# Gated mix of two attentions: single PSUM banks in the query stage, 72 instead of 80 maxima units in the front, and projections between two visits

## The chip, the cores and the metric

The kernel runs on one core of one Trainium2 chip. The metric is the device time of one execution in microseconds; the median of three runs is compared.

## The reference

Both halves get the same `x` of 2048 tokens by 448 columns, with 16 heads of 28.

```python
g = sigmoid((x * gate_w).sum(-1, keepdims=True))
# A: linear attention with a learned feature map
q, k, v = heads(x @ A_wqkv)
pq, pk = q @ w_phi, k @ w_phi                      # per head, 28 x 28
phi = concat([softmax(p), softmax(-p)])            # of pq and of pk: 56 features
kv, z = phi_k^T @ v, phi_k.sum(tokens)
a = ((phi_q @ kv) / (phi_q @ z + 1e-6)) @ A_wo
# B: full softmax attention
q, k, v = heads(x @ B_wqkv)
b = (softmax(q @ k^T * 28**-0.5) @ v) @ B_wo
out = g * a + (1 - g) * b
```

## The kernel before

The program is written for one core. The order of instructions on TensorE (PE), VectorE (DVE), ScalarE (ACT) and GpSimd (POOL) is the order of the Python code, written out by hand; DMAs go through the queue of SyncE (SP), which issues in its own order and waits in place. An engine that waits for one instruction holds all that are behind it.

The 16 heads are four groups `g` of four heads; the 2048 queries are four blocks `qb` of 512. A pair `gq = 4 g + qb` is the unit of attention B, so there are 16 of them, and one takes 16 steps `s` of 128 keys.

**Maxima.** The softmax of B subtracts the maximum of each query's scores over all keys, which has to be known before attention reaches that `gq`. So scores are computed twice, and the first time only their maxima are kept, as columns of `part`, 64 columns to a `gq`. This is done in two ways:

- In the front, as *units* (`mx_unit`, 16 to a `gq`, `NF` = 80 in all, the first five `gq`). A unit makes four matmuls of 512 keys: two into `pmb` (scores of the first block of keys) and two into `pmd` (scores of the difference of two blocks of keys, which `pair_load` prepares: DMAs bring `kp` and `kt`, POOL subtracts, line 189). ACT takes the relu of `pmd` into `rl` (line 245), DVE adds `pmb` and takes the maximum (line 248, two instructions). `rl` has one buffer; `pmb` and `pmd` each take two PSUM banks, from a ring of two such pairs (tag `mx`).
- In attention, as *visits* (`mx_visit`). A visit makes three matmuls of 512 keys into the three banks of `pm` (line 276, one buffer) and one DVE reduction over them (line 287).

When a `gq` is complete, `mx_reduce` reduces its columns on DVE, the next unit or visit transposes them on PE (`mx_done`), and ACT multiplies by -1 into `nm` (line 219). A visit with such a transpose has only two matmuls. A DMA puts `nm` into row 0 of the stack of queries `qst` (line 705, in `load_q`), where attention uses it as one more row of the contraction.

**The front** runs, one after the other:

1. Twenty projections `pqk` of B's queries and keys (line 494), written to DRAM as `qkd`.
2. The *key stage*, `t` from 0 to 15: `pk` (A's keys through the feature map, weights folded in line 326), `pva` (A's values), every second `t` a further `pqk`, and in pairs `kv_add`. A unit stands before and one after `pk`; for `t` of 3, 8 and 13 there is a third at the end (line 633).
3. The *query stage*, `q = t - 16` from 0 to 24. For each of 16 tiles of 128 tokens: `pq` (line 615), then features (`features1`: ACT copies to `pc`, DVE takes maximum and minimum, POOL and, for `q` below 7, DVE subtract in lines 382 and 384; ACT's exp in the next tile; `features2`: DVE's sum and reciprocal, POOL's product in line 395). Three tiles on, `turn` transposes the features on PE into `pft` (line 451), and ACT copies them to `fT` (line 453). Every second tile, `numer` computes numerators and denominators `pn` (line 462); `normalize1` has ACT copy them to `oU` (line 336, two buffers) and DMAs fetch the denominators; `normalize2` (DVE, DMAs) and `normalize3` (DVE, line 356) follow in the next tiles; `normalize4` splits the result into `oT` (ACT line 364, POOL line 365). `out_a` projects it (`poa`), and in the next tile `out_a2` has ACT multiply by the gate and stores it to `gad`. Units stand after `pq`, from `q` = 11 also in every second tile at the end, from `q` = 18 in each. From `q` = 18 on `value_b` computes B's values (`pvb`).
4. The rest of `value_b`, with a unit each, while POOL clears the stacks `qst` and `kst` (lines 691 and 693) and SP loads them. Units left over follow (line 722).

PSUM in the front is one pool of eight banks: three single banks `s` (for `pk`, `pva`, `pqk`, `pq`, `poa`, `pvb` and small ones), one `pv` for `pkv`, and two pairs `mx`, which units share with `pft` and `pn`.

**Attention.** A step makes four score matmuls into two pairs of banks `st` (line 754), two exps on ACT into `p` (line 756), a visit, and `values` (line 766) with `p` of the step before. In the last group (`g` = 3, from step 192) two projections by `woB` are worked in: `project_first` (nine matmuls, `pob_False`) at `kt` of 4, 6, 8 and 10, and `project_last` (three, `pob_True`) eleven steps and more after the end of a `gq`. They take one pair of banks from the ring of `st`. ACT multiplies the result by the gate and POOL adds it (lines 790, 791), or DVE does both (line 783). They stand after `values`; the step with a `project_first` then has a second visit:

```python
        mx_visit()
        if 0 < s <= NS:
            values(s - 1)
            ...
        for fn in late.pop(s, []):
            fn()
        if s in pobs and kt in FIRST:
            mx_visit()
```

Of the kernel before, what the change touches and what calls it, by code (L numbers as in the profile page):

```python
# [23 lines left out]
NG = 4  # L24
# [5 lines left out]
NF = 80  # L30
# [9 lines left out]
def gated_mix_kernel(ctx, tc, xT, wqkB, wvB, wvA, wkAT, wqAT, phi, woA, woB,  # L40
# [103 lines left out]
    mxs = {"u": 0, "f": 4 * NF, "fin": [], "pend": None}  # L144
# [57 lines left out]
    def mx_reduce(gq, n):  # L202

        def reduce():
            red = mxp.tile([P, 16], F32, tag="red", name=f"red{gq}", bufs=2)
            nc.vector.tensor_reduce(
                red.rearrange("p (h t) -> p h t", t=4),
                part[:, 64 * gq:64 * gq + 16 * n].rearrange("p (k t h) -> p h t k", t=4, h=4),
                AX.X, ALU.max)
            mxs["red"], mxs["pend"] = red, gq  # L210

        mxs["fin"].append(reduce)

    def mx_done(pt):

        gq, mxs["pend"] = mxs["pend"], None
        nc.tensor.transpose(pt[:16, :P], mxs["red"], ident)
        nm_of[gq] = nm = mxp.tile([16, P], F32R, tag="nm", name=f"nm{gq}", bufs=7)
        acts.append(lambda: nc.scalar.mul(nm, pt[:16, :P], -1.0))

    def mx_unit():

        u = mxs["u"]
        if u == NF:
            return
        if mxs["pend"] is not None:
            mx_done(ps_s(f"pt{mxs['pend']}"))
# [12 lines left out]
        for j in range(4):  # L240
            js = slice(32 * j, 32 * j + DH)
            nc.tensor.matmul((pb if j < 2 else pd)[:, j % 2, :], qc[js, qt * P:(qt + 1) * P],  # L242
                             kc[js, :], start=True, stop=True, tile_position=(32 * j, 0))
        rl = mxp.tile([P, 2, 512], F32, tag="rl", name=f"rl{u}", bufs=1)
        nc.scalar.activation(rl, pd, AF.Relu)  # L245
        col = 64 * gq + 16 * b + 4 * qt + 2 * hp
        for i in range(2):
            nc.vector.tensor_tensor_reduce(rl[:, i, :], pb[:, i, :], rl[:, i, :], 1.0, LOWEST,  # L248
                                           ALU.add, ALU.max, part[:, col + i:col + i + 1])
        if qt == 3 and gq + 1 == NF // 16:  # L250
            mx_load(g + (qb == NQ - 1), c)
        elif qt == 3 and qb == NQ - 1:
            pair_load(g + 1, c)
        if r == 15:
            mx_reduce(gq, 2)

    def mx_visit():
# [5 lines left out]
        n = min(3 if pend is None else 2, 4 * NU - f)  # L263
        if n <= 0 and pend is None:
            return
        mxs["f"] = f + n
        pm = ps2.tile([P, 3, 512], F32, tag="mx", name=f"pm{f}", bufs=1)
        for i in range(n):
            u, j = divmod(f + i, 4)
            gq, r = divmod(u, 16)  # L270
            g, qb = divmod(gq, NQ)
            kb, qt = divmod(r, 4)
            if r == 4 and j == 0 and gq + 1 < NG * NQ:
                mx_query(gq + 1)
# [6 lines left out]
            if r == 15 and j == 3:  # L281
                mx_reduce(gq, 4)
        if pend is not None:
            mx_done(pm[:, 2, :])
            acts.pop()()
        if n:
            nc.vector.tensor_reduce(part[:, f:f + n], pm[:, :n], AX.X, ALU.max)  # L287
# [45 lines left out]
    def normalize1(pool, pn, nm, n):  # L333

        oU = pool.tile([P, n, 512], F32, tag="oU", name=f"oU{nm}", bufs=2)
        (nc.scalar.copy if n == 2 else nc.vector.tensor_copy)(oU, pn)
# [106 lines left out]
    def turn(u):  # L443
# [4 lines left out]
        pt = ps_mx(f"pft{u}")  # L448
        f = fq.pop(u)
        for n in range(8):  # L450
            nc.tensor.transpose(pt[:112, n // 4, n % 4 * P:(n % 4 + 1) * P],
                                f[:, n * 112:(n + 1) * 112], ident)
        nc.scalar.copy(fT_of[tb][:, :, tl * P:(tl + 1) * P],
                       pt[:112].rearrange("p i (n q) -> p (i n) q", q=P))

    def numer(tb):

        pn = ps_mx(f"pn{tb}")
        for g in range(NG):
            for hh in range(2):  # L460
                n = 2 * g + hh
                nc.tensor.matmul(pn[64 * hh:64 * hh + 64, g // 2, g % 2 * 256:g % 2 * 256 + 256],
# [127 lines left out]
    for i in range(2 * NT + 9):  # L590
# [17 lines left out]
        if t < NT:  # L608
# [3 lines left out]
            mx_unit()  # L612
# [15 lines left out]
        if t < NT:  # L628
# [12 lines left out]
        if q == 2:  # L641
# [5 lines left out]
            kvT = kv_copy()  # L647
            woA_s = weights(3, "woA_s")
# [28 lines left out]
    out_a2(NT - 1)  # L677
    mx_fin()
# [23 lines left out]
    def load_q(gq):  # L702
        g, qb = divmod(gq, NQ)
        qst_of[gq] = r = load_stack(qst[gq % 2], q_d[g], qb * 512, (0, 0, 1, 1))
        nc.sync.dma_start(f32(r[0:1].rearrange("p a b -> p (a b)")), f32(nm_of.pop(gq)))
# [8 lines left out]
    load_q(0)  # L714
    for t in range(7, NT):
# [27 lines left out]
    pv_of, pts, late = {}, {}, {}  # L743
    pobs = set()
# [58 lines left out]
    def finish(gq, s):  # L803
# [5 lines left out]
        def f1():  # L809
            st["n"] = normalize1(late_p, pv_of[gq].unsqueeze(1), f"b{gq}", 1)  # L810
# [19 lines left out]
        if g == NG - 1:  # L830
            for tl in range(4):
                pobs.add(s + 11 + tl)
                late.setdefault(s + 11 + tl, []).append(
                    lambda tl=tl: project_last(qb, st["o"], tl, qb == 2))
# [34 lines left out]
    for s in range(NS + 16):  # L869
        take_acts()  # L870
        if s < NS:
# [21 lines left out]
        if s in pobs and kt in FIRST:  # L893
            mx_visit()
# [68 lines left out]
```

## Time and profile before

| | |
|---|---|
| Timed runs | 1160.21, 1160.40, 1161.12 us, median 1160.4 |
| Profiled execution | 1162.2 us, span 1160.4 us |
| Granted TensorE clock, mean | 0.976 |
| Busy in the span | PE 1092.5, ACT 743.6, DVE 689.0, POOL 248.6 us |
| Key stage, first `pk` to first `pq` | 66.5 to 206.9 us |
| Query stage to its last `out_a` | 206.9 to 399.9 us |
| Last values, to the first `st` of attention | 399.9 to 432.9 us |
| Attention | 432.9 us to the end |

Times within the trace are microseconds from the start of the span. An engine's busy time counts its instructions, not its waits; a matmul's duration overlaps the next one's, so the step from one start to the next is what a matmul costs PE. PEld is the loading of weights, which overlaps PE. In a list of instructions the bracket gives the idle time of the engine ahead of that instruction and what ended it. PEclk is the share of the full TensorE clock that was granted.

### The profile page before, as it was taken

The numbers are of one execution on the slowest core, as the hardware profiler recorded it, in microseconds if no ns is written. First come the engines' busy times: TensorE is split into PE (matmuls) and PEld (weight loads), VectorE is DVE, ScalarE is ACT, GpSimd is POOL, SyncE is SP. The second block draws the span as 40 slices with busy tenths as digits, with TensorE's granted clock in tenths as the row PEclk, the third lists the DMA queues.
The fourth block names the chain that finished last, engine by engine and source line by source line (L and its number), as shares of the span: only waits on it lengthen the run. The fifth ranks groups of instructions, "written<-read, shape, count | busy, mean of one in ns | idle before, by whom it ended". The sixth has DMA issues, their size and how long they took to land.

```text
span 1160.4 us, 16421 instructions
## 1 busy us (share of the span) xinstructions
PE 1092.5 (94%) x6360; PEld 591.2 (51%) x6360; DVE 689.0 (59%) x841; ACT 743.6 (64%) x876; POOL 248.6 (21%) x211
## 2 busy tenths in 40 slices
PE   7999999878889999999999999999999999999997
PEld 5877777656656763334333433333333344444443
DVE  4546767785444446767666676766676666654012
ACT  3445555565555556777777777777777766666763
POOL 1144444445562440011000000000000001121200
PEclk9999999999888998999999999999999999999999
DMA  8863101012122282143353221343322422122301
GB/s 259 297 182 97 46 27 45 19 45 70 45 75 83 83 176 55 39 130 111 74 117 84 66 69 37 80 101 83 88 56 58 115 52 76 40 79 82 118 10 64
DMA packets 64717, 99.56 MB, mean 86 GB/s; under 512 B 15456, under 2 KB 24528, under 8 KB 64640
## 3 DMA queue, kind: packets, MB, share of 16 engines
q1 hardware_dynamic: 64640, 98.52, 30.2%
q8 instruction: 50, 0.82, 0.3%
q14 instruction: 27, 0.22, 0.1%
HBM read 69.54 MB, written 28.57 MB: 85 GB/s over the span
## 4 chain that ended last, share of the span: by engine, by line
PE 81%; DVE 6%; ACT 5%; POOL 3%; issue 3%; DMA 1%; SPq 1%; ACTq 0%; POOLq 0%; DVEq 0%
PE st L754 22%; PE pv L766 21%; PE pm L276 9%; PE pqk L104 6%; PE pva L104 3%; PE pk L104 3%; PE pvb L104 3%; PE pob_False L104 3%; DVE part L287 2%; PE pmb L242 2%; PE poa L104 2%; PE pq L104 2%; POOL oTa L365 1%; PE pob_True L104 1%; ACT rl L245 1%
## 5 line engine op out<-in xcount | busy, mean ns | idle before, releaser
L756 ACT ACTIVATE p<-st 128x1024 f32<-128x1024 f32 x512 | 497.6, 1021 | 160.8 <-PE st L754 159.2
L287 DVE TENSOR_REDUCE part<-pm 128x3 f32<-128x1536 f32 (+1 forms) x239 | 413.3, 1729 | 200.9 <-PE pm L276 179.9
L754 PE MATMUL st<-qst,kst 128*128 128x512 f32 x1024 | 312.7, 424 | 6.0 <-DVE acc L783 2.6
L754 PEld LDWEIGHTS st<-qst,kst 128*128 128x128 f32 x1024 | 173.0, 189 | 231.1 <-ACT p L756 183.8
L766 PE MATMUL pv<-p,vb 128*32 128x512 f32 x2048 | 273.8, 606 | 0.0
L248 DVE CUSTOM_DVE_ANT_0 rl<-pmb,rl 128x512 f32<-128x512 f32 x160 | 103.2, 682 | 76.4 <-ACT rl L245 76.1
L276 PE MATMUL pm<-kc,qc 28*128 28x512 f32 x704 | 120.8, 497 | 9.3 <-DVE part L287 8.7
L245 ACT ACTIVATE rl<-pmd 128x1024 f32<-128x1024 f32 x80 | 82.2, 1028 | 36.2 <-PE pmd L242 32.9
L356 POOL TENSOR_TENSOR oUb<-oUb,rsb 128x512 f32<-128x512 f32 x15 | 19.3, 1283 | 388.8 <-DMA rsb<-rdb 274.7
L276 PEld LDWEIGHTS pm<-kc,qc 28*128 28x128 f32 x704 | 45.0, 182 | 97.8 <-DVE part L287 86.9
L104 PE MATMUL pqk<-XH,wB 128*128 128x512 f32 x224 | 70.9, 409 | 6.7 <-ACT XH L303 6.7
L766 PEld LDWEIGHTS pv<-p,vb 128*32 128x32 f32 x2048 | 40.5, 108 | 65.3 <-issue 60.1
L242 PE MATMUL pmd<-kp,qp 28*128 28x512 f32 x160 | 42.2, 517 | 14.1 <-DVE part L248 8.3
L104 PEld LDWEIGHTS pqk<-XH,wB 128*128 128x128 f32 x224 | 43.3, 196 | 16.3 <-ACT XH L303 6.9
L104 PE MATMUL poa<-woA_s,oTa 128*128 128x448 f32 x192 | 49.0, 409 | 0.1
L242 PE MATMUL pmb<-kp,qp 28*128 28x512 f32 x160 | 40.8, 505 | 6.7 <-ACT rl L245 3.5
L496 ACT CAST ev<-pqk 128x512 fp32r<-128x512 f32 x28 | 16.4, 587 | 46.7 <-PE pqk L104 44.4
L104 PEld LDWEIGHTS poa<-woA_s,oTa 128*128 128x128 f32 x192 | 39.2, 211 | 8.0 <-issue 4.3
L497 DVE TENSOR_TENSOR ev<-pqk,ev 128x512 fp32r<-128x512 f32 x28 | 19.4, 692 | 38.1 <-ACT ev L496 38.0
L104 PE MATMUL pk<-wkA_s,XH 128*128 128x448 f32 x128 | 40.1, 396 | 0.0
L791 POOL TENSOR_TENSOR acc<-acc,ob_False 128x448 f32<-128x448 f32 x12 | 13.7, 1142 | 122.5 <-ACT ob_False L790 122.5
L104 PE MATMUL pq<-wqA_s,XH 128*128 128x448 f32 x128 | 39.7, 393 | 0.0
(132 smaller groups left out, 1111.9 us busy)
## 6 DMA issues: line engine op xcount, KB each, us to landing
qkd<-ev SPq DMA_DIRECT2D x28, 512.0 KB
qst<-qkd SPq DMA_DIRECT2D x64, 224.0 KB
kst<-qkd SPq DMA_DIRECT2D x64, 224.0 KB
od<-oTb SPq DMA_DIRECT2D x12, 512.0 KB
oL<-od SPq DMA_DIRECT2D x12, 512.0 KB
xraw<-in_xT_dram SPq DMA_DIRECT2D x8, 512.0 KB
rsa<-rda SPq DMA_DIRECT2D x16, 256.0 KB
rsb<-rdb SPq DMA_DIRECT2D x15, 256.0 KB
```

The costliest lines, as they stand in the source:

```text
L104: nc.tensor.matmul(dst, l, r, start=i == 0, stop=i == len(todo) - 1)
L242: nc.tensor.matmul((pb if j < 2 else pd)[:, j % 2, :], qc[js, qt * P:(qt + 1) * P], kc[js, :], start=True, stop=True, tile_position=(32 * ...
L245: nc.scalar.activation(rl, pd, AF.Relu)
L248: nc.vector.tensor_tensor_reduce(rl[:, i, :], pb[:, i, :], rl[:, i, :], 1.0, LOWEST, ALU.add, ALU.max, part[:, col + i:col + i + 1])
L276: nc.tensor.matmul(pm[:, i, :], mxs[("qc", gq)][js, qt * P:(qt + 1) * P], mxs[("kc", g, kb)][js, :], start=True, stop=True, tile_position= ...
L287: nc.vector.tensor_reduce(part[:, f:f + n], pm[:, :n], AX.X, ALU.max)
L356: (nc.gpsimd if n == 1 else nc.vector).tensor_mul(oU, oU, rs)
L496: nc.scalar.copy(e[:, 0, :], pq)
L497: nc.vector.tensor_sub(e[:, 1, :], pq, f32(e[:, 0, :]))
L754: nc.tensor.matmul(st[:, jl, :], kst_of[(g, kt // 4)][:, j, (kt % 4) * P:(kt % 4 + 1) * P], qst_of[gq][:, j, :], start=True, stop=True)
L756: nc.scalar.activation(p, st, AF.Exp, scale=SCALE)
L766: nc.tensor.matmul(pv[32 * j:32 * j + 32, :], vb[kt // 8][:, kt % 8, 4 * g + j, :], pt[j // 2][:, j % 2, :], start=kt == 0, stop=kt == NT ...
```

## The change

- `NF` is 72. The front covers four `gq` in the old way and half of the fifth: its eight units take the query tiles `qt` 0 and 1 of all keys, and the visits take the rest (list `flats`, 736 matmuls instead of 704).
- The key stage has no unit before `t` = 2 and no third units; `pair_load` of the third and fourth pair comes at `t` = 1 and 3, and POOL's subtractions (`take_subs`) come behind the features of the tile.
- From `q` = 2 a new PSUM pool `psq` has four single banks and the two pairs. `turn` and `numer` take two single banks each, with one ACT copy for each bank; the pairs are left to the units. The pools wait tile by tile (`reuse_waits="tile"`).
- `oU` has three buffers in the query stage. DVE's share of the features' subtraction goes to POOL for all `q`. `out_a2` follows `out_a` in the same tile. The second unit of a tile stands in each tile from `q` = 14.
- In attention `nm` is multiplied by DVE. Its DMA is taken out of `load_q` (`load_nm`), and comes at `kt` = 12, or 14 for the last two `gq`. The second stack `qst1` is cleared last.
- `project_first` stands between the two visits of its step, ahead of `values`; `project_last` stands there too, and a second visit follows where the maxima are behind a schedule that ends in step 237.

```diff
-NF = 80
+NF = 72
...
-    ps = ps_s_.enter_context(tc.tile_pool(name="ps", bufs=1, space=PSUM))
+    ps = ps1 = ps_s_.enter_context(tc.tile_pool(name="ps", bufs=1, space=PSUM, reuse_waits="tile"))
...
-        return ps.tile([P, 512], F32, tag="s", name=nm, bufs=3)
+        return ps.tile([P, 512], F32, tag="s", name=nm, bufs=3 if ps is ps1 else 4)
...
-    def mx_done(pt):
+    def mx_done(pt, eng):
...
-        acts.append(lambda: nc.scalar.mul(nm, pt[:16, :P], -1.0))
+        if eng is nc.vector:
+            eng.tensor_scalar_mul(nm, pt[:16, :P], -1.0)
+        else:
+            acts.append(lambda: eng.mul(nm, pt[:16, :P], -1.0))
...
-        c, qt = divmod(r, 4)
-        hp, b = divmod(c, 2)
-        if r in (4, 9) and u // 16 + 1 < NF // 16:
-            pair_query(gq + 1, r // 9)
-        if r == 4 and gq + 1 == NF // 16:
-            mx_query(gq + 1)
+        if gq < GM:
+            c, qt = divmod(r, 4)
+            hp, b = divmod(c, 2)
+            col = 64 * gq + 16 * b + 4 * qt + 2 * hp
+            if r in (4, 9):
+                pair_query(gq + 1, r // 9)
+        else:
+            qt, c = divmod(r, 4)
+            hp, b = divmod(c, 2)
+            col = 64 * gq + 8 * b + 4 * qt + 2 * hp
+            if r == 0:
+                mx_query(gq)
...
+    flats = [(GM, kb, qt, h, 64 * GM + 16 + 8 * kb + 4 * (qt - 2) + h)
+             for kb in range(4) for qt in (2, 3) for h in range(4)]
+    flats += [(gq, kb, qt, h, 64 * gq + 16 * kb + 4 * qt + h) for gq in range(GM + 1, NG * NQ)
+              for kb in range(4) for qt in range(4) for h in range(4)]
...
-            mx_done(pm[:, 2, :])
-            acts.pop()()
+            mx_done(pm[:, 2, :], nc.vector)
...
-        oU = pool.tile([P, n, 512], F32, tag="oU", name=f"oU{nm}", bufs=2)
-        (nc.scalar.copy if n == 2 else nc.vector.tensor_copy)(oU, pn)
+        oU = pool.tile([P, n, 512], F32, tag="oU", name=f"oU{nm}", bufs=1 + n)
+        for i in range(n):
+            (nc.scalar.copy if n == 2 else nc.vector.tensor_copy)(oU[:, i, :], pn[i])
...
-        pt = ps_mx(f"pft{u}")
+        pt = [ps_s(f"pft{u}_{i}") for i in range(2)]
...
-        pn = ps_mx(f"pn{tb}")
+        pn = [ps_s(f"pn{tb}_{i}") for i in range(2)]
...
-        take_subs()
-        if t in (0, 1):
-            pair_load(0, 2 + t)
-        if 1 <= t < NT:
+        if 3 <= t < NT:
             mx_unit()
...
-            mx_unit()
+            if t >= 2:
+                mx_unit()
...
-            fq[q] = features1(pq, f"q{q}", nc.vector if q < 7 else nc.gpsimd)
+            fq[q] = features1(pq, f"q{q}", nc.gpsimd)
...
+        if i >= 1:
+            take_subs()
+        if t in (1, 3):
+            pair_load(0, 2 + t // 2)
...
-            if t in (3, 8, 13):
-                mx_unit()
         take_lows()
-        if 0 <= y - 9 < NT:
-            out_a2(y - 9)
...
+            ps_s_.close()
+            ps = ps_s_.enter_context(tc.tile_pool(name="psq", bufs=1, space=PSUM, reuse_waits="tile"))
...
             out_a(y - 8)
+            out_a2(y - 8)
...
-        if q >= NT + 2 or q >= 10 and q % 2:
+        if q >= NT - 2:
             mx_unit()
...
-        nc.sync.dma_start(f32(r[0:1].rearrange("p a b -> p (a b)")), f32(nm_of.pop(gq)))
+    def load_nm(gq):
+        nc.sync.dma_start(f32(qst_of[gq][0:1].rearrange("p a b -> p (a b)")), f32(nm_of.pop(gq)))
...
-    qst = [stack(f"qst{i}", False) for i in range(2)]
+    qst = [stack("qst0", False)]
     kst = [stack(f"kst{i}", True) for i in range(5)]
+    qst.append(stack("qst1", False))
...
+            if kt == (12 if gq + 1 < 14 else 14) and gq + 1 < NG * NQ:
+                load_nm(gq + 1)
...
-            if g == NG - 1 and kt in FIRST:
-                pobs.add(s)
-                late.setdefault(s, []).append(
-                    lambda qb=qb, tl=FIRST.index(kt): project_first(qb, tl, qb == 3))
...
         mx_visit()
+        if s < NS and g == NG - 1 and kt in FIRST:
+            project_first(qb, FIRST.index(kt), qb == 3)
+            mx_visit()
+        if s in mids:
+            mids.pop(s)()
+            if mxs["f"] * 237 < len(flats) * s:
+                mx_visit()
...
-        if s in pobs and kt in FIRST:
-            mx_visit()
```

More of the change, by code (lines that the diff above doesn't have):

```diff
@@ L200, in mx_fin, with mx_reduce @@
             mxs["fin"].pop(0)()
-    def mx_reduce(gq, n):
+    GM = NF // 16
+    def mx_reduce(gq):
+        col = 64 * gq
+        if gq < GM:
+            parts = [(0, 4, col, 2)]
+        elif gq == GM:
+            parts = [(0, 2, col, 2), (2, 4, col + 16, 4)]
+        else:
+            parts = [(0, 4, col, 4)]
         def reduce():
             red = mxp.tile([P, 16], F32, tag="red", name=f"red{gq}", bufs=2)
[L206 to L209, printed above, removed]
+            for a, z, c, n in parts:
+                nc.vector.tensor_reduce(
+                    red.rearrange("p (h t) -> p h t", t=4)[:, :, a:z],
+                    part[:, c:c + 4 * (z - a) * n].rearrange("p (k t h) -> p h t k", t=z - a, h=4),
+                    AX.X, ALU.max)
             mxs["red"], mxs["pend"] = red, gq
         mxs["fin"].append(reduce)
-    def mx_done(pt):
+    def mx_done(pt, eng):
         gq, mxs["pend"] = mxs["pend"], None
@@ L262, in mx_visit @@
         f = mxs["f"]
-        n = min(3 if pend is None else 2, 4 * NU - f)
-        if n <= 0 and pend is None:
+        todo = flats[f:f + (3 if pend is None else 2)]
+        todo = [x for i, x in enumerate(todo) if x[4] == todo[0][4] + i]
+        if not todo and pend is None:
             return
-        mxs["f"] = f + n
+        mxs["f"] = f + len(todo)
         pm = ps2.tile([P, 3, 512], F32, tag="mx", name=f"pm{f}", bufs=1)
-        for i in range(n):
-            u, j = divmod(f + i, 4)
-            gq, r = divmod(u, 16)
+        for i, (gq, kb, qt, j, col) in enumerate(todo):
             g, qb = divmod(gq, NQ)
-            kb, qt = divmod(r, 4)
-            if r == 4 and j == 0 and gq + 1 < NG * NQ:
-                mx_query(gq + 1)
+            if kb == 1 and qt in (0, 2) and j == 0 and gq + 1 < NG * NQ:
+                if ("qc", gq + 1) not in mxs:
+                    mx_query(gq + 1)
             js = slice(32 * j, 32 * j + DH)
@@ L280, in mx_visit @@
                 mx_load(g + 1, kb)
-            if r == 15 and j == 3:
-                mx_reduce(gq, 4)
+            if kb == 3 and qt == 3 and j == 3:
+                mx_reduce(gq)
         if pend is not None:
-            mx_done(pm[:, 2, :])
-            acts.pop()()
+            mx_done(pm[:, 2, :], nc.vector)
+        n = len(todo)
         if n:
-            nc.vector.tensor_reduce(part[:, f:f + n], pm[:, :n], AX.X, ALU.max)
+            col = todo[0][4]
+            nc.vector.tensor_reduce(part[:, col:col + n], pm[:, :n], AX.X, ALU.max)
     bd_s = ExitStack()
@@ L714, in gated_mix_kernel @@
     load_q(0)
+    load_nm(0)
     for t in range(7, NT):
@@ L742, in gated_mix_kernel @@
     NS = NG * NQ * NT
-    pv_of, pts, late = {}, {}, {}
-    pobs = set()
+    pv_of, pts, late, mids = {}, {}, {}, {}
     def scores(s, i):
```

34 lines of the change are left out of this document (16 added, 18 removed).

## The prediction

> **What bounds the kernel now.** I read the page's busy shares, then busy time by window, then the waits and the order in time of the stages that the change touches. The profiled execution took 1162.2 us for a span of 1160.4; the three timed runs have a median of 1160.4, so I sum against 1162.2 and take off 1.8 at the end. A change under 0.2% (2.3 us) counts as none.
>
> ```profile
> PE 1092.5 (94%) x6360; PEld 591.2 (51%) x6360; DVE 689.0 (59%) x841; ACT 743.6 (64%) x876; POOL 248.6 (21%) x211
> ```
>
> ```profile
> 160.00:180.00 20.00, 20.00 (x160) 15.27 (x159) 14.18 (x32) 10.98 (x18) 8.95 (x8) 1.00 0.15 54
> ...
> 240.00:260.00 20.00, 14.78 (x97) 11.11 (x99) 18.75 (x37) 14.25 (x19) 9.59 (x8) 1.00 0.24 64
> ...
> 320.00:340.00 20.00, 16.29 (x78) 11.44 (x77) 11.05 (x26) 10.59 (x15) 11.74 (x11) 0.83 0.21 65
> 340.00:360.00 20.00, 17.62 (x80) 12.10 (x80) 6.04 (x17) 8.68 (x11) 9.57 (x10) 0.76 0.28 91
> ...
> 460.00:480.00 20.00, 20.00 (x120) 7.84 (x118) 13.57 (x9) 15.12 (x16) 0.00 (x0) 1.00 0.10 23
> ```
>
> Columns: length, busy PE, PEld, DVE, ACT, POOL, granted clock. The key stage (66.5 to 206.9) and attention (from 432.9) are PE's. The query stage between is nobody's, except DVE's at 240; its clock sinks to 0.76. What holds it:
>
> ```profile
> ACT oUa L336 <- POOL oTa L365: 18.0, 4, 6.5
> ```
>
> ```profile
> PE pft L451 <- ACT rl L245: 9.2, 8, 1.3
> PE pmd L242 <- DVE part L248: 5.7, 6, 1.4
> ```
>
> ACT copies numerators only when POOL has read the oU two blocks back, and behind it stand the copies of pft; both hold pairs of banks that the maxima need.
>
> **Key stage.** Three extra units (t of 3, 8, 13) stand right before the next unit:
>
> ```profile
> 143.88 0.50 PE L242 MATMUL pmb<-kp,qp 28*128 28x512 f32 x2
> 144.01 0.50 PE L242 MATMUL pmd<-kp,qp 28*128 28x512 f32 x2
> 145.68 0.50 PE L242 MATMUL pmb<-kp,qp 28*128 28x512 f32 x2 [1.17 <-ACT rl L245]
> 147.02 0.50 PE L242 MATMUL pmd<-kp,qp 28*128 28x512 f32 x2 [0.84 <-DVE part L248]
> 147.46 0.67 PE L104 MATMUL pk<-wkA_s,XH 128*128 128x448 f32 x2
> ```
>
> Two take 3.58 us. An undisturbed pair of tiles, 158.18 to 173.51, is 15.33 us: two pk (2.43), two pva (2.45), pqk 2.57, kv_add 0.93 and four units, so 0.52 a unit. At these rates the stage holds 38.9 + 39.2 + 20.6 + 6.5 (seven kv_adds) + 4.2 (folds, one pt) + 34 x 0.52 = 127.1 us; it took 140.35. The 13.2 over are these doubles, 3.2 us in which the first unit's pmd waits for POOL's kp (68.84 to 72.52), and half-rate matmuls behind them. The change has 27 units, the first at t = 2, none doubled: 127.1 - 3.6 = 123.5, gain 16.9. Against that, POOL subtracts kp behind the features, SP's kt of the next pair waits for that, and wtq queues behind kt. Estimate: kp_0 done at 81.3, wtq's first slab at 85, its fold due at 84: 1 us. **Gain 15.5**, bounds 12 and 18.
>
> **Query stage, q 0 to 8** (a tile is one q; 206.86 to the turn at 262.36, 55.5 us). PE needs 9 pq (2.43), 9 units, 6 turns (0.84), 3 numer (1.88), kv_add and pkvT: 38.8. DVE needs 9 times ext 1.15, sum and reciprocal 1.42, unit 1.37, and 9.8 once (last key sum 1.4, ev 0.7, KV 0.7, gates 1.2, two splits of woA 3.4, normalizing 2.3): 45.3. Before, seven L384 of 0.94 made it 51.8; the change gives them to POOL, also at 0.94, whose 3.6 us a tile fit. PE's unit waits for DVE's one before. Taking 47: **gain 8.5** (4 to 11).
>
> **q 9 to 15** (262.36 to 334.01, 71.65 us). With a third oU, pft and pn in single banks and the pairs left to units, ACT no longer waits for POOL nor PE for ACT's copies. PE's work: 7 turns 5.9, 7 pq 17.0, 9 units 4.7, 7 out_a (2.64) 18.5, 3 numer 5.6, sum 51.7; 3.0 for two units that come too soon behind another. Cover: POOL a tile is 3.6, plus 2.5 of oT every second, of 7.5; ACT 5.5 of 7.5, its split copies costing two fixed starts (448 columns took 0.53, 1024 took 1.01, so 0.1 a pair). ACT's ga now waits in the same tile for out_a; behind it stand oU's copies, whose numer comes later on PE anyway. Four single banks come round after four allocations; each reader, all on ACT, is then a PE block of 2 us or more behind: nothing. The fall-back is a wait of 1 us a tile, 7. **Gain 17** (8 to 19).
>
> **q 16 to 18** (334.01 to 365.85, 31.84 us). PE: 2.5 + 3.1 + 7.9 + 3.8 + 2.5 (pvb) = 19.8. But two units a tile now stand with only a turn between: 3.58 - 1.04 = 2.5 each as in the doubles, three times, 7.5, and half-rate matmuls behind:
>
> ```profile
> 347.42 2.72 PE L104 MATMUL poa<-woA_s,oTa 128*128 128x448 f32 x12
> ...
> 354.66 4.85 PE L104 MATMUL poa<-woA_s,oTa 128*128 128x448 f32 x12
> ```
>
> 2.1 us lost on one block; I allow 3. **Gain 1.5** (-3 to 6). The Trainium skill, "TensorE: Matmul & The Clock Gate", section "Part 1: The HAM clock gate", has the clock halve after an idle window of about 3.4 us; the pft at 351.75 and 334.01 stood idle only 1.2 us ahead of slow blocks, so the trace does not keep to that length. By the page's length this stage would gain 4.5, not 1.5.
>
> From q 19 on a tile takes 6.15, and 3.03 in the loop of value blocks: both PE's, unchanged. The last doubled unit (429.4 to 432.85) goes: **gain 3.4** (2 to 3.5). POOL's memsets (19.9 us from the last out_a) and the K loads still end inside that loop's 27 us; moving qst1 last brings kst forward. One pair fewer is subtracted on POOL (the loop of value blocks doesn't take it), 2.6 us off the path.
>
> **Attention.** A step with a visit is 2.556, without 2.24. In the built program there are 250 visits instead of 239: they end in step 234 instead of 229.
> - nm: its multiplication moves from ACT to DVE.
>
> ```profile
> 498.49 1.23 DVE L287 TENSOR_REDUCE part<-pm 128x2 f32<-128x1024 f32 x1 [2.00 <-ACT nm L219]
> 499.77 0.51 PE L276 MATMUL pm<-kc,qc 28*128 28x512 f32 x3 [0.25 <-DVE part L287]
> ```
>
> The step after is 2.88 instead of 2.556; DVE's own 0.25 fits. Nine times 0.33: gain 3.0.
> - Eight first projections with visits (steps 196 to 218): now 8.37 a pair of steps, with PE idle behind the second visit:
>
> ```profile
> 949.27 0.50 PE L276 MATMUL pm<-kc,qc 28*128 28x512 f32 x3 [0.73 <-DVE part L287]
> ```
>
> That goes, but the projection, now ahead of values, needs the bank of its own step's first exp: exp starts 0.83 behind st and takes 1.0, PE is there 1.56 behind st, so 0.32 lost. 5.33 + 2.556 a pair: gain 3.8.
> - Steps 219 to 222: three second visits, each 0.85 behind DVE's reduction: 4.9 instead of 3.75, loss 3.3.
> - Steps 228 to 239: 41.7 now (1055.11 to 1096.83), 45.5 with three pairs as above, step 234 at 5.2 and four last projections at 3.56 instead of 3.31: loss 3.8.
> - Steps 244 to 254 have no visits: the projection waits 0.75 for exp instead of 0.33 for ob: loss 2.6.
> - The first three steps took 11.4 instead of 7.7 behind the doubled unit: gain 1.5.
>
> SP: load_nm has its own place two steps ahead of its use; behind one out store it issues a step before, and a step covers the landing. **Loss 1.4** together (6 to a gain of 3).
>
> **Sum.** 15.5 + 8.5 + 17 + 1.5 + 3.4 - 1.4 = 44.5: 1162.2 - 44.5 = 1117.7, less 1.8: **1116**. All bounds bad give 17 (1143), all good 59 (1101).
>
> **Rivals.**
> - Waits move, not go: out_a waits for POOL's oT, or ACT stands at ga while features queue. For it: POOL sits 10.1 us before one oT at 346. Half of q 0 to 15 is lost, 12.8: 1129, spread 1127 to 1143. Chance 0.18.
> - Projections wait for the second exp of their step: 1.0 more in 28 steps, 28: 1144. Against: two banks alternate, and the first is the older. 0.05.
> - The change frees no bank that matters, since unit waits for unit through the one pair and the one rl; only the key stage and the tail gain: 1160.4 - 18.9 = 1142. Against: of PE's 31 us of waits there, 23 are those of pft and pn for a pair, or of units for their copies. 0.05.
> - Slower: the query stage stays at a lowered clock. Short waits between units remain, transposes are many, and 340:360 shows 0.76. It decides if PE's work of that stage, 38.8 + 51.7 + 19.8 + 36.9 (q 19 to 24) = 147 us, runs below 0.77: 147 x (1/0.77 - 1) = 44 eats all gains; at 0.72 it loses 57: 1173. Against: the key stage, with as many small pauses, shows 1.00. The same skill page, section "A second HAM failure mode: psum-queue depth-cycling", tells of a kernel whose clock swings because PE pauses at each PSUM hand-over; by it this rival would be the rule, and the 1.00 at 160:180 speaks against. 0.05.
>
> Forecast 0.65 (1104 to 1127), same 0.02. Faster: 0.65 + 0.18 + 0.05 + 0.05 = 0.93; slower 0.05. Leaving out the clock rival and the cases at 1142 and 1144, the range is 1101 (all bounds good) to 1140.
>
> **What would show it.** pk to pq starting 15 us earlier with no kp wait; oUa without a wait for POOL; turns 7.5 us apart from q 9 to 15, clock near 1.00; waits of pmb for rl left at q 16 to 18; steps of 2.56 behind each nm. If turns stay 10 us apart, or steps 235 to 254 pass 4 us, I am wrong.

## The result and the profile after

The changed kernel takes 1119.4 us (median of four runs, 1117.4 to 1121.8) where the kernel before takes 1160.8: a ratio of 0.964, with a 95% interval of 0.962 to 0.966. The forecast was 1116, the range 1101 to 1140. The profiled execution took 1119.7 us for a span of 1117.9.

From the order in time on PE (first `pk`, first `pq`, turns of q 9 and 16, first scores, end) the span divides as follows. All stage times below are read at these points, in one execution of each kernel; gains are taken before rounding.

| us | before | after | gain | forecast |
|---|---|---|---|---|
| up to the first `pk` | 66.5 | 65.0 | 1.5 | 0 |
| key stage | 140.4 | 124.0 | 16.3 | 15.5 |
| q 0 to 8 | 55.5 | 45.3 | 10.2 | 8.5 |
| q 9 to 15 | 71.6 | 57.8 | 13.9 | 17 |
| q 16 to the first scores | 98.8 | 91.5 | 7.3 | 4.9 |
| attention | 727.5 | 734.3 | -6.8 | -1.4 |
| span | 1160.4 | 1117.9 | 42.5 | 44.5 |

The first row is code that the change doesn't touch; in the fourteen traces of this document it takes 63.9 to 66.5 us, and 65.0 in e5, which has the code of before there; so its 1.5 us are chance. The busy line and windows of the page and trace of the changed kernel (windows: length, busy PE, PEld, DVE, ACT, POOL, granted clock, DMA share, GB/s):

```profile
PE 1074.5 (96%) x6360; PEld 580.8 (52%) x6360; DVE 696.2 (62%) x826; ACT 736.7 (66%) x880; POOL 254.6 (23%) x216
```

```profile
160.00:180.00 20.00, 20.00 (x161) 15.32 (x159) 14.05 (x34) 10.53 (x17) 8.95 (x8) 1.00 0.21 64
240.00:260.00 20.00, 18.42 (x98) 14.74 (x97) 11.89 (x24) 12.01 (x18) 14.16 (x12) 0.91 0.31 98
292.00:312.00 20.00, 17.01 (x87) 11.39 (x85) 9.93 (x27) 12.17 (x18) 4.47 (x4) 0.83 0.23 73
...
340.00:360.00 20.00, 20.00 (x103) 15.55 (x103) 7.65 (x24) 10.77 (x15) 8.68 (x8) 1.00 0.22 72
```

PE has 18 us less of busy time for as many matmuls. An estimate: some 14 of it is the clock, since by the clock records of the traces TensorE ran at half rate for 30.5 us after and for 57.9 us before. The stages have moved: the line at 240 is now q 9 to 12, that at 292 is q 16 to 18 (0.83 where before, at 340, it was 0.76), and the one at 340 is q 22 and later. The 18 us in which ACT's copies of `oU` waited for POOL are gone; these copies now wait for PE, and shortly. What ACT waits for longest is `poa` at `ga`, since `out_a2` follows `out_a` in the same tile (engine, line, releaser: us, times, longest, from 235 to 320 us):

```profile
ACT ga L506 <- PE poa L104: 14.3, 8, 4.4
...
ACT oUa L364 <- PE pn L491: 3.3, 10, 0.7
```

What PE still waits for between 60 and 400 us (the five longest; none names `ga`):

```profile
PE pmd L264 <- DVE part L269: 5.8, 8, 1.1
PE pm L302 <- DMA kc<-qkd: 3.0, 1, 3.0
PE pft L479 <- POOL featq L410: 1.6, 1, 1.6
PE poa L104 <- POOL oTa L393: 1.6, 1, 1.6
PE pq L104 <- ACT oUa L364: 1.3, 1, 1.3
```

Line 1 is for the larger part (3.9 of 5.8) the units of q 14 to 18, where two stand close together in each tile. Line 2 is new, and is the first visit of attention. Lines 4 and 5 are one event in q 9. DVE came to its normalizing 1.85 us before the broadcast `rsa` had landed, ACT's copies and POOL's `oT` followed late, and PE paused twice. That `rsa` is slower than before isn't shown: from its issue on SP to DVE's use are 8.4 us (225.4 to 233.8) after the change, and 9.3 us (247.1 to 256.4) before, where DVE didn't wait. PE then ran ten `poa` matmuls in 3.26 us. In e6 (below), with the same code in this stage, the same two pauses stand there, and ten take 2.33:

```profile
236.75 0.67 PE L104 MATMUL pq<-wqA_s,XH 128*128 128x448 f32 x2 [1.34 <-ACT oUa L364]
...
241.87 3.26 PE L104 MATMUL poa<-woA_s,oTa 128*128 128x448 f32 x10 [1.58 <-POOL oTa L393]
```

and in e6:

```profile
236.05 0.67 PE L104 MATMUL pq<-wqA_s,XH 128*128 128x448 f32 x2 [1.44 <-ACT oUa L364]
...
241.18 2.33 PE L104 MATMUL poa<-woA_s,oTa 128*128 128x448 f32 x10 [1.56 <-POOL oTa L393]
```

### The profile page after: what moved, and what is told of

It is laid out like the page before. It is cut to its first block, busy times and chain, and to the rows that moved or that the text cites. A ratio compares the mean times of both kernels' runs of the same rounds, so it can differ in the third digit from the quotient of the medians.

```text
span 1117.9 us, 16433 instructions
## 1 busy us (share of the span) xinstructions
PE 1074.5 (96%) x6360; PEld 580.8 (52%) x6360; DVE 696.2 (62%) x826; ACT 736.7 (66%) x880; POOL 254.6 (23%) x216
## 4 chain that ended last, share of the span: by engine, by line
PE 84%; ACT 3%; DVE 3%; DMA 3%; POOL 3%; issue 2%; SPq 0%; ACTq 0%; POOLq 0%; DVEq 0%
PE st L785 25%; PE pv L797 23%; PE pm L302 9%; PE pqk L104 6%; PE pk L104 3%; PE pva L104 3%; PE pob_False L104 3%; PE poa L104 3%; ACT p L787 2%; PE pmb L264 1%; PE pq L104 1%; PE pvb L104 1%; PE pn L491 1%; PE pob_True L104 1%; DMA kc<-qkd 1%
## 5 line engine op out<-in xcount | busy, mean ns | idle before, releaser
L314 DVE TENSOR_REDUCE part<-pm 128x3 f32<-128x1536 f32 (+1 forms) x250 | 431.8, 1727 | 188.2 <-PE pm L302 188.2
L785 PE MATMUL st<-qst,kst 128*128 128x512 f32 x1024 | 309.0, 423 | 0.0
L302 PE MATMUL pm<-kc,qc 28*128 28x512 f32 x736 | 126.7, 497 | 5.1 <-DMA kc<-qkd 3.0
L269 DVE CUSTOM_DVE_ANT_0 rl<-pmb,rl 128x512 f32<-128x512 f32 x144 | 92.7, 682 | 55.8 <-ACT rl L267 55.6
L302 PEld LDWEIGHTS pm<-kc,qc 28*128 28x128 f32 x736 | 47.5, 182 | 95.8 <-DVE part L314 78.3
L267 ACT ACTIVATE rl<-pmd 128x1024 f32<-128x1024 f32 x72 | 73.9, 1026 | 9.8 <-PE pmd L264 6.9
L104 PEld LDWEIGHTS pqk<-XH,wB 128*128 128x128 f32 x224 | 42.1, 191 | 16.4 <-ACT XH L330 7.4
L525 ACT CAST ev<-pqk 128x512 fp32r<-128x512 f32 x28 | 16.4, 587 | 44.7 <-PE pqk L104 42.3
L264 PE MATMUL pmd<-kp,qp 28*128 28x512 f32 x144 | 36.8, 499 | 6.0 <-DVE part L269 5.8
L393 POOL TENSOR_TENSOR oTb<-oUb,oTb 128x512 fp32r<-128x512 f32 x15 | 19.2, 1279 | 88.2 <-ACT oTb L392 88.2
L104 PE MATMUL pob_False<-woB_s,oL 128*128 128x448 f32 x144 | 33.6, 377 | 5.5 <-ACT p L787 5.5
```

The lines of the kernel that those rows point to most:

```text
L104: nc.tensor.matmul(dst, l, r, start=i == 0, stop=i == len(todo) - 1)
L302: nc.tensor.matmul(pm[:, i, :], mxs[("qc", gq)][js, qt * P:(qt + 1) * P], mxs[("kc", g, kb)][js, :], start=True, stop=True, tile_position= ...
L314: nc.vector.tensor_reduce(part[:, col:col + n], pm[:, :n], AX.X, ALU.max)
L393: nc.gpsimd.tensor_sub(oT[:, 1, :], oU[:, k, :], f32(oT[:, 0, :]))
L785: nc.tensor.matmul(st[:, jl, :], kst_of[(g, kt // 4)][:, j, (kt % 4) * P:(kt % 4 + 1) * P], qst_of[gq][:, j, :], start=True, stop=True)
```

## Experiments

Unless said otherwise, a kernel is the changed one with one edit. "Tail" is from the turn of q 16 to the first scores, "start" from there to the values of step 3 (within attention). A ratio is to executions of the kernel before made together with that kernel (their medians were 1159.4 to 1161.6), so it isn't the quotient of two lines of the table.

| kernel | median us | ratio to before (95%) | key | q 0-8 | q 9-15 | tail | start | attention |
|---|---|---|---|---|---|---|---|---|
| before | 1160.8 | 1 | 140.4 | 55.5 | 71.6 | 98.8 | 15.6 | 727.5 |
| after | 1119.4 | 0.964 (0.962-0.966) | 124.0 | 45.3 | 57.8 | 91.5 | 16.3 | 734.3 |
| e1_two_oU | 1135.6 | 0.979 (0.976-0.982) | 124.0 | 46.5 | 73.6 | 93.2 | 13.1 | 730.3 |
| e2_pairs | 1135.9 | 0.979 (0.976-0.981) | 124.4 | 53.9 | 56.5 | 101.7 | 13.6 | 731.4 |
| e3_dve_sub | 1120.8 | 0.967 (0.963-0.970) | 124.1 | 47.3 | 55.8 | 90.6 | 16.3 | 733.5 |
| e4_k_doubles | 1121.8 | 0.967 (0.964-0.969) | 135.3 | 45.4 | 56.5 | 87.8 | 11.9 | 729.0 |
| e5_before_oU3 | 1150.5 | 0.992 (0.990-0.994) | 141.3 | 55.5 | 62.1 | 98.3 | 15.5 | 727.7 |
| e6_proj_late | 1111.9 | 0.960 (0.958-0.962) | 124.2 | 45.3 | 56.5 | 90.4 | 16.6 | 729.0 |
| e7_kc_early | 1117.7 | 0.963 (0.961-0.965) | 123.9 | 46.3 | 56.4 | 89.1 | 15.8 | 732.4 |
| e8_nm_act | 1123.3 | 0.968 (0.966-0.971) | 124.3 | 43.8 | 58.0 | 92.0 | 16.0 | 738.4 |
| e9_unit_first | 1118.1 | 0.964 (0.961-0.967) | 124.0 | 45.3 | 56.2 | 90.7 | 19.0 | 736.8 |
| e10_all | 1111.9 | 0.958 (0.955-0.961) | 124.0 | 45.3 | 56.3 | 96.9 | 12.0 | 722.7 |
| e11_sub_dve | 1106.5 | 0.954 (0.952-0.956) | 124.1 | 45.3 | 56.7 | 90.4 | 12.0 | 723.4 |
| e12_spread | 1106.4 | 0.953 (0.950-0.955) | 125.6 | 45.3 | 59.8 | 86.7 | 12.0 | 722.7 |

An edit's price is read from its stage. Where the code of a stage is that of the changed kernel, the key stage took 123.9 to 125.6 us, q 0 to 8 43.8 to 46.3, and q 9 to 15 56.2 to 58.0, so a difference of 2 us in one stage isn't shown by its length alone.

### The third buffer: e1_two_oU and e5_before_oU3

```diff
-        oU = pool.tile([P, n, 512], F32, tag="oU", name=f"oU{nm}", bufs=1 + n)
+        oU = pool.tile([P, n, 512], F32, tag="oU", name=f"oU{nm}", bufs=2)
```

> The changed kernel with two buffers of the numerators' copy oU instead of three; everything else as changed. Theory (the third buffer is what took the waits away from turns 9 to 18): ScalarE's copies of oU wait again for GpSimd's oT of the pair before, the ring of oT waits comes back, the stretch from turn 9 to unit 319 (85.1 us in the profile of the changed kernel) takes 10 us more (4 to 14), the whole time 1129 us (1123 to 1133). Rival (the single banks alone freed these turns): the stretch grows by under 3 us, 1119 to 1122 us.

q 9 to 15 grew by 15.8 us, to 73.6: longer than before the change. The wait is back on ACT, and PE stood 16.4 us behind those copies at `pq`. Before the change `pn` lay in a pair, and what PE waited for these copies in that stage was 2.7 us, at `pmb`; now `pq` takes its bank from the same ring of four as `pn`, so it is `pq` that a late copy holds. From 240 to 330 us of e1:

```profile
ACT oUa L364 <- POOL oTa L393: 21.1, 5, 6.8
```

e5 is the kernel before with the opposite edit alone (`bufs=2` to `bufs=1 + n`):

> The kernel before with three buffers of oU instead of two and nothing else. Theory (the third buffer works by itself): turns 9 to 15 take 9 us less (5 to 15) of the 71.7 us that they took, the whole 1151 us (1145 to 1156). Rival (the third buffer takes effect only where ScalarE and the turns do not wait for shared pairs and for VectorE's subtractions, so it needs the rest of the change): turns 9 to 15 within 3 us of before, 1158 to 1161 us.

It gained 9.6 us in the same seven turns, and there the wait for `oT` is no longer among the longest of ACT. So the buffer works by itself, and the gain of q 9 to 15 needs it: with everything else and without it, that stage gained nothing. The theory held in both runs; in e1 the price is above its upper bound of 14. The single banks have no part in this gain, as q 9 to 15 took 56.5 us without them too (e2, below). Between e5 (62.1) and e2 lie 5.6 us that come from other edits of the change. What the traces show in that stage is one unit fewer in e2 than in e5, and another clock (granted 1.00 and 0.94, with PE busy for 51.3 and 55.9 us); no run takes these edits apart.

### Single banks: e2_pairs

```diff
-        pt = [ps_s(f"pft{u}_{i}") for i in range(2)]
+        pm = ps_mx(f"pft{u}")
+        pt = [pm[:, 0, :], pm[:, 1, :]]
...
-        pn = [ps_s(f"pn{tb}_{i}") for i in range(2)]
+        pn2 = ps_mx(f"pn{tb}")
```

> The changed kernel with pft and pn in the pairs of banks of the maxima again, one copy each, as before the change; oU keeps three buffers, the features stay on GpSimd, units stay where they are. Theory (oU was the main thing in turns 9 to 15, the banks the smaller one): queries 0 to 18 take 5 us more (2 to 10), 1124 us (1121 to 1129). Rival (the shared pairs were what held the turns): 15 us more, 1134 us or later.

16 us slower, so the theory's 5 was far too little, and by the median the rival was right. But the place is another than either said: q 9 to 15 did not lose (56.5), q 0 to 8 lost 8.6 and the tail 10.2. In the tail PE waited 7.9 us, 3.0 after the change; 2.6 of it is a wait of the first scores for the maxima of the last unit, 2.5 are two waits of turns. And by the clock records it ran there at half rate for 17.1 us, 6.8 after the change, which makes some 5 us more (an estimate: half of the difference). PE's waits in e2 from 188 to 300 us:

```profile
PE pft L482 <- DVE part L269: 4.5, 4, 1.6
PE pft L482 <- ACT rl L267: 4.5, 4, 1.3
PE pn L494 <- ACT rl L267: 3.5, 3, 1.2
```

Where a turn stands right behind a unit (q 0 to 8, q 16 on) it waited for that unit's readers; from q 9 `out_a` lies between. Buffer and banks thus work in different stages.

### VectorE's subtractions: e3_dve_sub

```diff
-            fq[q] = features1(pq, f"q{q}", nc.gpsimd)
+            fq[q] = features1(pq, f"q{q}", nc.vector if q < 7 else nc.gpsimd)
```

> The changed kernel with the second feature subtraction of queries 0 to 6 on VectorE again. Theory (VectorE is the bound of queries 0 to 8, so seven subtractions of some 0.75 us lengthen it one for one): queries 0 to 8 take 5 us more (3 to 6.6), 1124 us. Rival (by the profile of the changed kernel the stretch also waits for GpSimd's features, and this gives that wait back, or VectorE has slack): at most 1 us more or a gain of up to 2 us, 1117 to 1120 us.

q 0 to 8 took 2.1 us more than after the change, not 5, and the time did not move beyond its spread. The 2.1 alone would be within what the same code shows; but e3 had a granted clock of 1.00 in this stage, where the changed kernel had 0.96, and e8, with the changed kernel's code there and 1.00 too, took 43.8, 3.6 less than e3. So the seven subtractions of 0.94 (6.6 us) cost some 2 to 4: VectorE is not the bound of q 0 to 8 one for one.

### Third units in the key stage: e4_k_doubles

```diff
                 proj_qk(NP + t // 2, ev)
+            if t in (3, 8, 13):
+                mx_unit()
```

> The changed kernel with the third units of key tiles 3, 8 and 13 put back into the key stage; three units fewer are then left for the loop ahead of attention. Theory (three units too close together are what cost the key stage before: a wait of about 2.5 us each and slower matmuls behind it): the key stage takes 10 us more (6 to 12), the loop ahead of attention 2 us less, and the loads of kc come earlier, so that the 3 us wait of the first visit for them ends: in all plus 5 us, 1124 us (1120 to 1128). Rival (the units are hidden wherever they stand; the key stage gained by something else): the key stage unchanged within 3 us, 1113 to 1118 us.

The key stage took 11.3 us more, 3.8 a unit: the 0.52 of its matmuls, waits of 0.9 at the first of the three and of 2.0 at each of the others, and half rate behind the second (granted clock 0.83 from 130 to 150 us):

```profile
136.71 0.49 PE L264 MATMUL pmb<-kp,qp 28*128 28x512 f32 x2 [1.17 <-ACT rl L267]
138.05 0.79 PE L264 MATMUL pmd<-kp,qp 28*128 28x512 f32 x2 [0.85 <-DVE part L269]
138.78 1.11 PE L104 MATMUL pk<-wkA_s,XH 128*128 128x448 f32 x2
```

The last line is two `pk` matmuls that take 0.67 at full rate. Most of it (8.1 us) came back: the tail took 3.7 less, and the start of attention 4.4 less, as the last unit then lies three value tiles ahead. In sum 2.4 us slower by the medians, within the two spreads.

### Projections behind the values: e6_proj_late

```diff
         if s < NS and g == NG - 1 and kt in FIRST:
-            project_first(qb, FIRST.index(kt), qb == 3)
-            mx_visit()
+            if mxs["f"] < len(flats):
+                project_first(qb, FIRST.index(kt), qb == 3)
+                mx_visit()
+            else:
+                late.setdefault(s, []).append(
+                    lambda qb=qb, tl=FIRST.index(kt): project_first(qb, tl, qb == 3))
```

and the same for `mids`.

> The changed kernel, in which the projections of steps without visits left (the last projections of steps 235 to 238 and 251 to 254, the first ones of steps 244 to 250) stand behind the step's value matmuls again. Theory (a projection ahead of the values makes TensorE wait for the second exponential, 0.39 us in each of 12 steps by the step lengths 3.71 and 4.94 after against 3.32 and 4.55 before): 4.7 us less (3 to 5.5), 1115 us. Rival (these steps are as long in either order, the loss lies in the clock or in loads): within 1 us of the changed kernel.

Attention took 5.4 us less, all of it from step 235 on. In the order in time of PE, a last projection after the change stood ahead of `pv` and waited for the exp of its own step. It is the first of the two, not the second that the theory names: it ended at 1042.11, the second at 1043.03.

```profile
1042.16 0.87 PE L104 MATMUL pob_True<-woB_s,oTb 128*128 128x448 f32 x3 [0.64 <-ACT p L787]
```

In e6 it comes behind `pv`, and what waits is half as long:

```profile
1035.38 0.87 PE L104 MATMUL pob_True<-woB_s,oTb 128*128 128x448 f32 x3
...
1037.03 0.73 PE L785 MATMUL st<-qst,kst 128*128 128x512 f32 x2 [0.32 <-ACT ob_True L821]
```

### The copy of nm: e8_nm_act

```diff
-            mx_done(pm[:, 2, :], nc.vector)
+            mx_done(pm[:, 2, :], nc.scalar)
+            acts.pop()()
```

> The changed kernel with the negation of the transposed maxima (nm) in attention on ScalarE again. Theory (ScalarE's copy makes the step behind it 0.33 us longer, VectorE's does not; 11 of them lie in attention): 3.3 us more (2 to 4), 1122 to 1123 us. Rival (the step is longer for the transpose and its wait, not for the copy's engine): within 1 us.

Attention took 4.1 us more. DVE's reduction waits for ACT's copy, which stands behind two exps, and the next visit waits for DVE:

```profile
420.93 1.23 DVE L315 TENSOR_REDUCE part<-pm 128x2 f32<-128x1024 f32 x1 [2.00 <-ACT nm L235]
...
422.21 0.50 PE L302 MATMUL pm<-kc,qc 28*128 28x512 f32 x3 [0.27 <-DVE part L315]
```

### The start of attention: e7_kc_early and e9_unit_first

After the change the first visit waited for `kc`, whose loads SP issues behind those of `kst`, and the matmuls behind it were slow:

```profile
387.71 1.17 PE L302 MATMUL pm<-kc,qc 28*128 28x512 f32 x3 [2.96 <-DMA kc<-qkd]
388.81 2.08 PE L785 MATMUL st<-qst,kst 128*128 128x512 f32 x4
```

e7 issues these loads earlier, e9 puts each value tile behind its unit:

```diff
-            qt, c = divmod(r, 4)
+            c, qt = divmod(r, 2)
```

> The changed kernel with the last eight units in another order, key chunk by key chunk (both blocks of 128 queries of a chunk next to each other), so that the loads of kc are issued two units apart, the first six units earlier. Theory (the first visit waited 2.96 us for the first kc, and the matmuls behind the wait ran at half rate for some 2 us): attention 4 us shorter (2.5 to 5.5), 1115 to 1116 us. Rival (something else is late next, such as VectorE's maxima of the last unit, or kst): the wait turns into another one, at most 1 us gained.

```diff
-        value_b(t)
         take_acts()
         mx_unit()
+        value_b(t)
```

> The changed kernel with one swap in the loop ahead of attention: each unit stands before its value tile instead of behind it, so that 2.5 us of value matmuls lie between the last unit and the first scores. Theory (what the start of attention loses is three things that all end with the last units: the loads of kc, ScalarE's relu and VectorE's maxima of the last unit, and the half rate of TensorE after waiting for any of them; the run with the third units in the key stage had its last unit three tiles earlier and its first three steps were 4.4 us shorter): the first three steps take 12 us (11.9 to 13.5) instead of 16.3, the loop itself as long as before, 1115 us. Rival (only the loads of kc count, which come just 3 us earlier here and still behind kst; or units next to the second unit of turn 24 lengthen the loop): under 1.5 us gained.

Neither did what its theory said. In e7 the wait for `kc` went, and 1.43 for ACT's exps and 0.75 for DVE's maxima took its place; the start took 15.8 us. In e9 the last unit was no longer in the way, but `kc` still came 2.60 late, and behind it and a further pause of 0.71 TensorE ran at half rate for 10.2 us (386.2 to 396.5): 19.0 us, longer than with the wait of 2.96.

```profile
384.43 0.82 PE L302 MATMUL pm<-kc,qc 28*128 28x512 f32 x3 [2.60 <-DMA kc<-qkd]
385.18 1.21 PE L785 MATMUL st<-qst,kst 128*128 128x512 f32 x4
387.10 0.80 PE L302 MATMUL pm<-kc,qc 28*128 28x512 f32 x3 [0.71 <-DVE part L314]
...
394.29 2.08 PE L785 MATMUL st<-qst,kst 128*128 128x512 f32 x4
```

### Together: e10_all, e11_sub_dve and e12_spread

e10 has the edits of e6, e7 and e9, and a second visit fewer beside last projections (`mxs["f"] * 238`). It also issues the eighth pair's subtraction (`take_subs()` in the loop ahead of attention), which the changed kernel leaves out. (Without it, a unit of that pair adds the relu of the second block's scores, not of the difference, so what it keeps is no maximum; the quotient of the softmax does not depend on the number subtracted.)

> The changed kernel with what the runs pointed to: projections behind the values where no visit is left, kc loaded chunk by chunk, the unit ahead of its value tile, one of the three second visits beside last projections (step 221) moved to the end of the visits, and the subtraction of the eighth pair of keys issued. Theory (the parts add: 5.3 us in attention by the projections, 4 at its start, 0.9 by the visit): a span of 1108 us, a time of 1109 us (1106 to 1112). Rival (the start of attention stays, since kc or the banks are late in any order): 1112 us, no better than the projections alone.

The start of attention fell to 12.0, so the two edits that missed alone work together: the visit waits neither for `kc` nor for the last unit, and the clock stays up. (In e10 the longer tail also gives `kc` more time; e11, without it, took 12.0 too.) Attention is 11.6 us shorter than after the change; the visit's share is the 0.9 us between e6 and e10 in steps 219 to 254. But the tail grew by 5.4 us. On POOL, the subtraction stood behind twelve memsets of stacks:

```profile
375.62 1.80 POOL L719 MEMSET qst<- 128x2048 f32 x1
377.49 2.59 POOL L189 TENSOR_TENSOR kp<-kp,kt 28x512 fp32r<-28x512 f32 x2
```

and a unit waited for it, 2.08 and then 0.84 us. e11 takes it from POOL's queue (against e10):

```diff
-        take_subs()
...
+        if t == 9:
+            subs.pop(0)(nc.vector)
```

> The kernel of e10_all with the eighth pair's subtraction on VectorE, after the third value tile of the loop ahead of attention. Theory (in e10_all that subtraction stood on GpSimd behind twelve memsets that ran from 355.8 to 377.4 us, so that the units of the pair waited 2.1 and 0.8 us for it and TensorE ran at half rate behind the waits; this is the whole of the 5.6 us by which the loop was longer): from the last turn to the first scores 75 us (74 to 76.5) again, a span of 1104.5 us, a time of 1106 us (1104.5 to 1108). Rival (the unit ahead of its value tile, or the other order of the last eight units, lengthens the loop): 80 us, 1111 us again.

The tail took 90.4 us again, and the time is 1106.5 us: 13 us less than the changed kernel by the medians, a margin that holds (intervals of the ratio 0.952 to 0.956, and 0.962 to 0.966). So it was the subtraction's place, and not the order of units, that lengthened the loop. e12 is e11 with second units moved:

```diff
-        if q >= NT - 2:
+        if 11 <= q < 16 or q >= 19:
```

> e11_sub_dve with the second units of queries 14 to 24 at queries 11 to 15 and 19 to 24: those of queries 16, 17 and 18 stand at 11, 12 and 13. Theory (two units a turn without a projection are bound by ScalarE's relu and VectorE's maxima, 2.5 us or more a unit; beside a projection they cost their matmuls, some 0.5 to 1 us): queries 16 to 18 take 5 us less (3 to 7), queries 9 to 15 take 2 us more (1 to 3.5), in all 3 us less, 1103 us. Rival (queries 9 to 15 are then bound by VectorE or by the waits that units bring, 2.5 us for each wherever it stands): nothing gained, 1106 us.

The tail took 3.6 us less and q 9 to 15 took 3.0 more; the medians are equal. A second unit costs some 1.2 us where it stood and 1.0 where it went: the rival's result, though its price of 2.5 us holds nowhere here.

## Why the prediction was right, and where it was not

**The sum was right to 2 us (42.5 for 44.5), by terms of which three were off and partly cancelled. That they cancelled is luck, and 1.5 of the 42.5 is the first row, which is no part of the forecast.**

- *Key stage (16.3 for 15.5).* Right, with its reason: 124.0 us against the 123.5 of its contents, `wtq` late by 1.2 (1 was allowed), `kp` by 0.3. e4 shows the third units as the larger part, 11.3 of the 16.3.
- *q 0 to 8 (10.2 for 8.5).* The size was near, the reason was not. I took DVE's sum (45.3) as the bound, and the seven subtractions as what lowered it from 51.8. That the stage then took 45.3 is chance: DVE was busy for 33.9 us of it (for 46.0 before, where my sum says 51.8). Columns as above:

```profile
189.04:234.32 45.28, 41.55 (x308) 31.58 (x300) 33.88 (x74) 32.10 (x48) 28.35 (x24) 0.96 0.13 40
```

e3 gives the subtractions 2 to 4 us; e2 gives the single banks 8.6. The stage was held by turns and numerators that waited for units' readers. Before, from 206.86 to 262.36, PE waited 12.0 us in all, of it:

```profile
PE pft L451 <- ACT rl L245: 4.5, 4, 1.3
PE pn L462 <- ACT rl L245: 3.5, 3, 1.2
```

After, it waits 3.7. The prediction saw the waits of `pft`, but booked them under q 9 to 15.
- *q 9 to 15 (13.9 for 17).* Right in its main cause, the third `oU` (e1, e5). Turns stood 8.3 us apart instead of 7.5. The sum allowed 3.0 of waits, for units; these took 1.4, but the two pauses of q 9 took 2.9, which the prediction did not see. They stand in the other runs too; the changed kernel's 57.8 against 56.2 to 56.5 in five runs is the half rate that followed them here, and not there. That the single banks help in this stage, as the sum says, is refuted by e2.
- *q 16 to 18 (4.5 for 1.5).* The doubled units were oversized: 2.5 each was read from a pair with nothing between, and here they cost 1.2 (e12). Their waits are 3.0 us in all, not 7.5, and most of it is 0.84 for DVE, not for `rl`. The 3 us for half-rate matmuls were about right: the clock was at 0.50 from 294.1 to 300.9. So the prediction's other figure, 4.5 with a clock that stays up, came out as a number and not for its reason.
- *From q 19 (2.8 for 3.4).* As forecast, the last doubled unit is gone.
- *Attention (-6.8 for -1.4).* The term that failed, by 5.4. Right or near: `nm` (steps 3 to 195 gained 2.6 of the 3.0; e8 gave back 2.9 there, and 1.7 in steps 219 to 222), the eight first projections with visits (84.4 to 81.5 us, 3.0 for 3.8), steps 219 to 222 (a loss of 3.1 for 3.3). Wrong by size: steps 228 to 239 lost 4.3 for 3.8, steps 240 to 254 lost 3.9 for 2.6, step 255 and the end lost 0.8, which the sum does not have; I had seen the wait for exp, but taken a last projection at 3.56, and it took 3.7 (e6 took back 5.3 of the 8.1 of steps 228 to 254). Wrong in sign: the first three steps, -0.8 for +1.5. I followed SP for `kst` and `qst`, and did not see that `kc` is now issued by the last four units, behind twelve `kst` loads.

Of the rivals, "waits move" came true at two places: in q 9, at 2.9 us, and at `kc`, at some 4, instead of 12.8. ACT did stand at `ga`, but no wait of PE names it. "Projections wait for the second exp" did not come true: all 27 projections that waited, 0.71 us at most, started 0.05 us after the first exp of their step, as the sum had it; in the 12 steps without a visit that cost 0.4 each. "No bank freed that matters" is refuted by e2 (16 us). The lowered clock stayed a matter of single places: 0.91 in the window with q 9, 0.83 in q 16 to 18, where it had been 0.76.

Two more points. One sign of being wrong was met to the letter: of steps 235 to 254, four took over 4 us (4.9 to 5.2); but the same four took 4.06 before. And the good bounds add up to 60.5, not 59, so the range would start at 1100.

Left open: which edits bring the 5.6 us between e5 and e2 in q 9 to 15, and why equal pauses are followed by half rate in one run and not in another.

## What to carry to other kernels

Where several engines pass buffers round, find for each stage which hand-over ends last, and test the edits stage by stage: here the kernel was 16 us slower without one buffer and 16 us slower without the single banks, in different stages, and the two medians alone would not have told the stages. When work is moved out of a stage, follow the transfers that its last instructions issue, on SP and on POOL too, since the next stage starts with them. And price a wait with the slow matmuls behind it: two half cures of the start of attention gained 0.5 and lost 2.7 us, and both together gained 4.4 (as did e4, whose last unit and `kc` loads come earlier).

## What the runs showed of the hardware

Pauses much shorter than I had thought were followed by half rate, and for longer than the pause. In e9, after a pause of 2.60 us and one of 0.71, `pm` took 0.80 instead of 0.50 and `st` 2.08 instead of 1.20; by the clock records the clock was at 0.50 from 386.2 to 396.5 us. The `st` right behind the longer pause still took 1.21. After the change, 2.96 us of pause went with half rate from 386.3 to 393.1. In e7, pauses of 1.43 and 0.75 went with 6.8 us of it; in e1, pauses of 1.44 and 0.76 at the same place with none. In q 9, pauses of 1.34 and 1.58 went with 3.4 us of it after the change, and 1.44 and 1.56 in e6 with none. In q 15 and 16 after the change, two pauses of 0.84 and 0.85 were followed by 6.8 us. So the length of a pause alone does not decide, and none of these was longer than 2.96 us.

The clock records of all fourteen traces show more: but for those that end with the trace, each of the 67 stretches at half rate lasts 3.41, 6.83 or 10.24 us, that is one, two or three times 3.41 (36, 26 and 5 of them). So a pause was followed either by no half rate at all or by at least 3.41 us of it, which is some 1.7 us of work not done (an estimate: half of 3.41).

The Trainium skill, "TensorE: Matmul & The Clock Gate", section "Part 1: The HAM clock gate", says that the activity window runs freely, about 3.4 us long; the 3.41 us of the stretches agree with that, and it would fit that equal pauses end differently. By it at least one busy window brings the full rate back. After the change one was enough (389.7 to 393.1); in e9 PE was busy throughout from 389.6 to 393.1, and the clock stayed at 0.50 for 3.4 us more.
